# Attention and two gated products on one core: state products on row tiles, the first batch's product and the second's attention put on the job list, and softmax scalings put on ScalarE

## The chip, the core and the metric

The kernel runs on one core of one Trainium2 chip. The engines are TensorE (PE, with its weight loads PEld), VectorE (DVE), ScalarE (ACT), GpSimd (POOL), and the queue SP that issues most of the transfers. The metric is device time in microseconds, of the whole launch, as the median of several runs. Lower is better.

## The reference, cut to what matters

```python
# x: 8 x 8 x 512 x 64, state: 8 x 8 x 32 x 64 (batch, head, rows, depth)
scores  = scale * x @ state.T            # read weights a  = softmax over the 32 state rows
scores2 = scale * state @ x.T            # write weights a2 = softmax over the 512 rows
                                         # both: exp(s - max) / (sum + 1e-9)
xread, sread = a @ state, a2 @ x
X = concat([xread, sread], rows)         # 8 x (512 + 32) rows, heads side by side: 4352 x 512
X = ((X @ w1) * (X @ w2)) @ w3 @ w_out   # 512 -> 1024 -> 1024 -> 512
out = ((X @ w_a) * (X @ w_b)) @ w_out2   # 512 -> 1536 -> 512
```

The weights arrive as 64-bit floats and are converted on the chip; the output is float32.

## The kernel before, in words

**Precision.** Most products run in a reduced format, fp32r, in three passes: an operand is split into a rounded part h and a remainder l, and h·h, h·l and l·h are summed (`PASSES`). One split is a cast on ACT and a subtraction on DVE or POOL (`split` L130; the rows name the parts `wkh`, `wkl`, `ah`, `al`). Small products run in plain fp32; each of these shows as two records in the trace.

**What is multiplied.** xread is never formed for the first product. Since xread @ w = a @ (state @ w), the kernel first makes p = state @ [w1, w2] per head (`state_product` L320, tile `pb`, moved to SBUF as `sg`), stores p to DRAM (`p_d`), loads it back in another layout (`pr`), splits it, and multiplies by the read weights: ap and bp are the two products of a batch, h = ap·bp. Also w3 @ w_out is formed once (`weight_product` L362, tile `wp`, result `ws`), so that x2 = h @ ws (tile `x2p`).

**Stage one, the job list, 0 to 154.5 us.** Weight loads, conversions (two operations on ACT, two on DVE, one on POOL for each half), state products for all eight batches, w3 @ w_out, and batch 0's attention are `Job`s (L610). `EARLY` (L24) orders the loads; `run_jobs` (L653) is a planner that places the jobs with costs written in the code, gives each to an engine, and thus fixes the order on each engine and on SP. PSUM's eight banks are divided: three for `pb`, two for transposed w3, one for `wp`, two for attention. The state is laid out block-diagonally (`bdh`, `bdl`, `bd`, six tiles that are first set to zero), so that one product of 128 rows handles two heads; there are 64 such products of three passes each.

**Stage two, batches 0 to 7, 154.5 to 631.4 us.** `block1` runs eight steps per batch. A step (L1085) is six passes into ap, a copy of ap on ACT, six into bp, a multiply on DVE (`hfp`), a split, and, one step late, twelve passes into x2p (L1130). Between the passes stand small pieces of the next batches' attention: the table `MIDDLE` (L534) says which TensorE pieces come after which step, `BEHIND` (L543) which moves on ACT and DVE. `scores` is the product with the state, `maxima` to `row_split` the two softmaxes, `read` the product a2 @ x. The last batch is interleaved with the product for the state rows. Weights of stage three are converted meanwhile (`Intake`, tasks `ab`, started at the steps of `AB_AT` L37).

**Stage three, from 631.4 us.** `block2` computes the second gated product in three-pass products.

## Time and profile before

| what | value |
|---|---|
| median of 3 runs | 1415.35 us (1412.34 to 1421.07) |
| profiled execution, its time | 1415.62 us |
| its span | 1413.9 us |
| granted TensorE clock, mean over the span | 0.977 of full speed |
| busy: PE, PEld, DVE, ACT, POOL | 1342.6, 1089.4, 758.8, 540.8, 431.9 us |

Busy time is counted on the profiled execution's span; matmuls overlap a little, so PE's busy share is not its share at peak rate. An engine's idle time costs something only where TensorE waits for it. The clock is given as a share of full speed: 1.00 is 2.4 GHz, 0.5 is 1.2 GHz.

### The profile page before, as it was taken

The page shows a single profiled execution, that of the slowest core. Times are in us where ns is not written, and L with a number is a line of the kernel's source. Part 1 is how long each engine was busy: PE and PEld are TensorE (multiplying, and loading weights), DVE is VectorE, ACT ScalarE, POOL GpSimd, SP SyncE. Part 2 cuts the span into 40 slices and gives each one's busy share as a digit, 9 for nine tenths or more (in the row PEclk, how much of TensorE's full clock was granted, in tenths as well). Part 3 has the DMA queues.
Part 4 walks back from the last instruction along what each step waited for, and adds up shares of the span by engine and source line. Part 5 has one row for each costly group of instructions (what it writes and reads, how often), then busy time and mean ns, then how long its engine had stood idle before and what let it go on. Part 6 is the DMA issues. An engine that isn't in the chain of part 4 may idle for free.

```text
span 1413.9 us, 17464 instructions
## 1 busy us (share of the span) xinstructions
PE 1342.6 (95%) x6596; PEld 1089.4 (77%) x6596; DVE 758.8 (54%) x979; ACT 540.8 (38%) x915; POOL 431.9 (31%) x292
## 2 busy tenths in 40 slices
PE   6599999999899999989999999999999999999998
PEld 3377777777677677878788888888888888888877
DVE  8997377686777577756652271222462223622241
ACT  7667445545445355535422141111331223322220
POOL 4544243533453336625530043111131011311110
PEclk8699999999999999999999999999999999999999
DMA  9689732944555555256754326543464443644401
GB/s 295 195 291 314 227 121 105 283 139 172 181 175 168 155 162 130 75 196 241 258 214 144 108 103 221 189 158 128 140 226 165 154 141 133 225 164 164 150 1 60
DMA packets 120612, 242.85 MB, mean 172 GB/s; under 512 B 43984, under 2 KB 64464, under 8 KB 120528
## 3 DMA queue, kind: packets, MB, share of 16 engines
q1 hardware_dynamic: 115952, 225.48, 48.8%
q0 software_dynamic: 4576, 16.26, 3.0%
q8 instruction: 52, 0.85, 0.2%
q14 instruction: 32, 0.26, 0.1%
HBM read 176.16 MB, written 65.54 MB: 171 GB/s over the span
## 4 chain that ended last, share of the span: by engine, by line
PE 64%; DVE 6%; issue 2%; ACT 2%; DMA 1%; POOL 0%; SPq 0%; DVEq 0%; ACTq 0%; POOLq 0%
PE o L1375 18%; PE r L1363 18%; PE v L1363 9%; PE q L1363 5%; PE x2p L1130 4%; PE abs L1418 2%; PE bp L1071 2%; PE ap L1071 2%; PE os L1447 1%; PE bs L1071 1%; DVE hfp L1095 1%; DMA z<-z_d 1%; DVE ab L167 1%; DVE hp L132 1%; DVE sw L167 0%
## 5 line engine op out<-in xcount | busy, mean ns | idle before, releaser
L1375 PE MATMUL o<-z,h 128*128 128x512 f32 x1152 | 276.8, 389 | 2.9 <-DMA z<-z_d 1.6
L1375 PEld LDWEIGHTS o<-z,h 128*128 128x128 f32 x1152 | 216.0, 188 | 49.0 <-DMA z<-z_d 2.0
L1538 POOL TENSOR_TENSOR hb<-e,e 128x512 f32<-128x512 f32 x48 | 62.4, 1300 | 467.5 <-DVE e L1388 467.5
L1130 PE MATMUL x2p<-hp,ws 128*128 128x512 f32 x768 | 188.3, 394 | 2.7 <-DVE hp L132 2.2
L131 ACT CAST h<-e 128x512 fp32r<-128x512 f32 x48 | 29.8, 620 | 375.2 <-DVE e L1541 361.3
L1130 PEld LDWEIGHTS x2p<-hp,ws 128*128 128x128 f32 x768 | 145.7, 191 | 35.1 <-DVE hp L132 3.3
L1388 DVE TENSOR_TENSOR e<-e,q 128x512 f32<-128x512 f32 x48 | 33.0, 688 | 197.9 <-PE q L1363 197.9
L132 POOL TENSOR_TENSOR pl<-pr,ph 128x1024 fp32r<-128x1024 f32 x32 | 78.7, 2458 | 136.0 <-ACT ph L131 101.1
L131 ACT CAST hp<-hfp 128x512 fp32r<-128x512 f32 x64 | 39.7, 620 | 124.1 <-DVE hfp L1095 120.9
L132 DVE TENSOR_TENSOR hp<-hfp,hp 128x512 fp32r<-128x512 f32 x64 | 56.8, 887 | 48.6 <-ACT hp L131 48.0
L1388 DVE TENSOR_TENSOR e<-e,v 128x512 f32<-128x512 f32 x48 | 33.0, 687 | 82.4 <-PE v L1363 82.4
L1095 DVE TENSOR_TENSOR hfp<-asbp,bp 128x512 f32<-128x512 f32 x64 | 43.5, 679 | 54.3 <-PE bp L1071 53.2
L1363 PE MATMUL r<-xT4h,w 128*128 128x512 f32 x192 | 67.1, 390 | 2.0 <-DVE e L1388 2.0
L1363 PE MATMUL r<-xT2h,w 128*128 128x512 f32 x192 | 67.1, 390 | 0.0
L1363 PE MATMUL r<-xB11h,w 128*128 128x512 f32 x192 | 66.9, 389 | 0.0
L1363 PE MATMUL v<-xT1h,w 128*128 128x512 f32 x192 | 66.9, 389 | 0.0
L1363 PE MATMUL r<-xT3h,w 128*128 128x512 f32 x192 | 66.9, 389 | 0.0
L1363 PE MATMUL q<-xB21h,w 128*128 128x512 f32 x192 | 66.9, 389 | 0.0
L1363 PE MATMUL v<-xB22h,w 128*128 128x512 f32 x192 | 66.9, 389 | 0.0
L1089 ACT COPY asbp<-ap 128x512 f32<-128x512 f32 x64 | 37.6, 587 | 68.4 <-PE ap L1071 68.0
L1071 PE MATMUL bp<-ah,ph 128*128 128x512 f32 x128 | 57.8, 452 | 2.2 <-ACT sr L529 1.7
L132 DVE TENSOR_TENSOR h<-e,h 128x512 fp32r<-128x512 f32 x48 | 34.5, 719 | 33.4 <-ACT h L131 33.4
(506 smaller groups left out, 2996.5 us busy)
## 6 DMA issues: line engine op xcount, KB each, us to landing
w<-w_d SPq DMA_DIRECT2D x172, 512.0 KB, 5.2
w_d<-w SPq DMA_DIRECT2D x48, 512.0 KB, 2.7
p_d<-sg SPq DMA_DIRECT2D x64, 256.0 KB, 4.7
pr<-p_d SPq DMA_DIRECT2D x32, 512.0 KB, 5.1
x<-in_x_dram SPq DMA_DIRECT2D x64, 128.0 KB, 3.5
x_d<-x2sp POOLq DMA_DIRECT2D x16, 512.0 KB, 5.4
sw<-in_moe_w_dram SPq DMA_DIRECT2D x32, 256.0 KB, 6.8
xB<-x_d SPq DMA_DIRECT2D x16, 512.0 KB, 4.7
```

The lines of the kernel that those rows point to most:

```text
L131: nc.scalar.copy(hi, src)
L132: (eng or nc.vector).tensor_tensor(out=lo, in0=src, in1=hi.bitcast(F32), op=ALU.subtract)
L167: nc.vector.scalar_tensor_tensor(out=out, in0=c, scalar=0x80000000, in1=out, op0=ALU.bitwise_and, op1=ALU.bitwise_or)
L1071: nc.tensor.matmul(dst[:, :n], lhsT=l[m], rhs=r[q], start=i == 0 and j == 0, stop=i == k - 1 and j == 2,)
L1089: nc.scalar.copy(a_sb[:, :n], pa[:, :n])
L1095: nc.vector.tensor_tensor(out=hf[:, :n], in0=a_sb[:, :n], in1=pb[:, :n], op=ALU.mult)
L1130: nc.tensor.matmul(acc[j], lhsT=w_s[f][:, m, j * P : (j + 1) * P], rhs=h[:, q, :n], start=per == 1 and f == 0 and i == 0, stop=f == NF1 - ...
L1363: nc.tensor.matmul(t, lhsT=w[m], rhs=xf[g].parts[x][q][:, k, :], start=first and k == 0 and i == 0, stop=k == 1 and i == 2, skip_group_che ...
L1375: nc.tensor.matmul(t, lhsT=h[:, m, part * P : (part + 1) * P], rhs=z_t[f][:, q, :], start=first and c == 0, stop=last and c == 2,)
L1388: nc.vector.tensor_tensor(out=out, in0=x, in1=y, op=ALU.add)
L1418: nc.tensor.matmul(t[:, w * 256 : (w + 1) * 256], lhsT=l[m], rhs=x_s[k][q], start=k == 0 and i == 0, stop=k == 3 and i == 2,)
L1538: nc.gpsimd.tensor_tensor(out=h2[-1][:, f % 2, :], in0=e2, in1=e5, op=ALU.mult)
```

## The change

- **State products.** The state is transposed, copied once to one tile `stT` and not split; w1 and w2 are not split either. A product has 64 rows in the contraction (one head), the two heads of a pair stand on rows 0 to 63 and 64 to 127 of the array and write two banks, in plain fp32: 64 products in 32 pairs. Those of batches 0 to 3 are made early; the 16 pairs of batches 4 to 7 are jobs of low priority, moved by ACT alone. The stores to `p_d` are 128 of 128 KB, where there were 64 of 256 KB.
- **Order and banks.** All eight PSUM banks are one pool. `EARLY` begins with w_out and w3, so w3 @ w_out is TensorE's first large work. `KEEP`, `STORE_BEHIND`, the tables of the `ab` tasks (six from the batches' steps where there were seven) and the planner's costs change too.
- **Job list.** Batch 0's whole product (`first_product`, `first_copy`, `first_mult`, `first_high`, `first_low`, `first_output`), batch 1's attention and batch 2's transposes of x become jobs; the loop over batches begins at 1. Of batch 0, x2 is made after all eight steps, in four runs of 24 passes (tile `x2f`).
- **Scores.** Eight products per batch, each 64 rows by 32 columns of the array, into two banks, all after step 1; before, four of 128 rows by 64 columns, two after step 0 and two after step 1.
- **Softmax.** The addition of 1e-9, the scale of the maximum (`nm`) and half of x's copies go to ACT; the write weights are no longer scaled on DVE (two operations, `e<-e,r`), but their product is, when ACT moves it (`sn`, two operations where there was one).
- **Splits on POOL** of 128x1024 become two of 512 columns.

```diff
 NUNITS = 47
-BANKS = dict(pb=3, wt=2, wp=1, at=2)
+BANKS = dict(ps=8)
...
 EARLY = (
-    "wk0_0 wk1_1 wk0_1 wo0 wo1 wo3 wo2 wk1_0 x0 w3_0 w3_1 "
-    "w3_2 wk2_0 x1 w3_3 wk2_1 wk3_1 wk3_0 w3_4 w3_5 w3_6 w3_7"
+    "wo1 wo3 wo0 w3_1 wo2 w3_2 w3_0 wk0_0 x0 wk1_0 wk2_0 w3_3 "
+    "w3_5 w3_6 x1 wk1_1 w3_4 wk3_0 wk0_1 x2 w3_7 wk3_1 wk2_1"
 ).split()
...
-KEEP = 5
+KEEP = 9
 KEEP_SG = 2
-STORE_BEHIND = 24
-
-
-
-AB_AT = {0: 1, 1: 7, 2: 13, 8: 19, 9: 25, 10: 31, 11: 37}
-AB_LATER = (3, 4, 5, 6, 7)
-AB_RESERVE = 5
+KEEP_UNTIL = 40
+STORE_BEHIND = 18
+
+LATE_KEEP = 6
+LATE_PRIO = 10
...
         nc.scalar.copy(hi, src)
-        (eng or nc.vector).tensor_tensor(out=lo, in0=src, in1=hi.bitcast(F32), op=ALU.subtract)
+        if eng is nc.gpsimd and len(src.shape) == 2 and src.shape[1] == 1024:
+            parts = [slice(i * 512, (i + 1) * 512) for i in range(2)]
+        else:
+            parts = [slice(None)]
+        for i in parts:
+            (eng or nc.vector).tensor_tensor(
+                out=lo[:, i], in0=src[:, i], in1=hi[:, i].bitcast(F32), op=ALU.subtract
+            )
...
 
...
-    def state_product(p, nh, bp, i):
-        if i == 0:
-            sg[p, nh, bp] = unit(f"sg{p}_{nh}_{bp}")
-        t = pb[p, nh, bp, i] = bank(f"pb{p}_{nh}_{bp}_{i}")
-        wk = pair("wk", f"{p}_{nh}")
-        for n, (l, m) in enumerate(PASSES):
+    def state_product(p, nh, bg, i):
+
+        for r in range(2):
+            if i == 0:
+                sg[p, nh, bg, r] = unit(f"sg{p}_{nh}_{bg}_{r}")
+            t = pb[p, nh, bg, i, r] = bank(f"pb{p}_{nh}_{bg}_{i}_{r}")
+            rows = slice(r * D, (r + 1) * D)
             nc.tensor.matmul(
                 t,
-                lhsT=bd_s[p // 2][l][:, p % 2, 2 * bp : 2 * bp + 2, :],
-                rhs=wk[m][:, half[i]],
-                start=n == 0,
-                stop=n == 2,
-            )
-
-    def state_move(p, nh, bp, i, eng):
-        dst = sg[p, nh, bp].rearrange("p (q w c) -> p q w c", q=2, w=2)[:, :, i, :]
-        src = flat(pb.pop((p, nh, bp, i)), 256)
+                lhsT=st_s[rows, (bg * NP + p) * P : (bg * NP + p + 1) * P],
+                rhs=conv[f"wk{p}_{nh}"].out[rows, half[i]],
+                start=True,
+                stop=True,
+            )
+
+    def product_move(p, nh, bg, i, r, eng):
+        dst = sg[p, nh, bg, r].rearrange("p (q w c) -> p q w c", q=2, w=2)[:, :, i, :]
+        src = flat(pb.pop((p, nh, bg, i, r)), 256)
         if eng == "A":
             nc.scalar.copy(dst, src)
         else:
             nc.vector.tensor_copy(dst, src)
 
...
     def recip(s, n, tag):
         r = sm.tile([P, n], F32, tag=tag, name=tag)
-        nc.vector.tensor_scalar(out=r, in0=s, scalar1=1e-9, scalar2=None, op0=ALU.add)
+        nc.scalar.activation(out=r, in_=s, func=AF.Identity, bias=eps, scale=1.0)
         nc.vector.reciprocal(out=r, in_=r)
...
-            nc.vector.tensor_copy(self.xt[g][:, 0, :], self.banks.pop((g, 0)))
+            nc.scalar.copy(self.xt[g][:, 0, :], self.banks.pop((g, 0)))
...
+        def scores(self):
+
+            for r in range(2):
+                self.banks[r] = bank(f"st{self.b}_{r}")
+            c = self.b // 4 * 512 + self.b % 4 * NS
+            for p in range(NP):
+                for r in range(2):
+                    rows = slice(r * D, (r + 1) * D)
+                    nc.tensor.matmul(
+                        self.banks[r][NS * p : NS * (p + 1), :],
+                        lhsT=st_s[rows, c + p * P : c + p * P + NS],
+                        rhs=self.xt[p // 2][rows, p % 2, :],
+                        start=True,
+                        stop=True,
+                    )
+            free(*(f"xt{self.b}_{g}" for g in range(2)))
...
+            nc.scalar.activation(out=self.nm, in_=mx, func=AF.Copy, scale=-SCALE)
...
+        def col_sums(self):
+            self.r2 = recip(self.sum2, 2, f"r2_{self.b % 4}")
...
+            t = self.banks.pop("r")
+            for g in range(2):
+                part = slice(g * D, (g + 1) * D)
+                nc.scalar.activation(
+                    out=self.sn[:, part], in_=t[:, part], func=AF.Copy, scale=self.r2[:, g : g + 1]
+                )
...
-        0: [(1, "scores", 0)],
-        1: [(1, "scores", 1)],
+        1: [(1, "scores")],
...
-        for bp in range(B // 2):
-            moves = []
+        for bg in range(1):
+            moves = {0: [], 1: []}
             for i in range(2):
                 pr = Job(
                     "P",
-                    0.65,
-                    lambda a=(p, nh, bp, i): state_product(*a),
-                    after=[lows[i], state_done[p // 2, bp // 2]] + last[-1:],
-                    need=1 - i,
+                    1.0,
+                    lambda a=(p, nh, bg, i): state_product(*a),
+                    after=[adds[i], state_moved[bg]] + last[-1:],
+                    need=2 - 2 * i,
                     keep=KEEP_SG,
                     prio=2 + len(loads) / 100,
-                    banks=("pb", 1),
+                    banks=("ps", 2),
                 )
                 last.append(pr)
...
+                for r in range(2):
+                    moves[r].append(
+                        Job(
+                            "AV",
+                            (0.6, 0.85),
+                            lambda e, a=(p, nh, bg, i, r): product_move(*a, e),
+                            after=[pr],
+                            prio=0,
+                        ).gives("ps", 1)
+                    )
...
+    def attention_jobs(b, done):
+        prio = 1 + 2 * b
+        a = attn[b]
+        t = Job("P", 1.3, a.scores, after=[*done, *state_moved.values()], prio=prio, banks=("ps", 2))
+        for g in range(2):
+            done.append(
+                Job("A", 0.6, lambda g=g: a.scores_move(g), after=[t] + done[2:], need=1 - g, prio=prio).gives("ps", 1)
+            )
+        mx = Job("V", 2.9, a.maxima, after=done[2:], need=1, prio=prio)
+        ce = Job("A", 1.3, a.col_exp, after=[mx], need=1, prio=prio)
+        rs = Job("V", 2.9, a.row_shift, after=[mx], prio=prio)
+        re = Job("A", 1.1, a.row_exp, after=[rs], prio=prio)
+        sc = Job("V", 0.3, a.col_sums, after=[ce], prio=prio + 2)
+        su = Job("V", 1.5, a.sums, after=[re], prio=prio)
+        ct = Job("P", 1.8, a.col_transpose, after=[ce], prio=prio + 2, banks=("ps", 2))
+        cm = Job("AV", (1.3, 1.4), lambda e: a.col_move(), after=[ct, sc], need=1, prio=prio + 2).gives("ps", 2)
+        rn = Job("V", 2.9, a.row_norm, after=[su], need=1, prio=prio)
+        sp = Job("A", 1.1, a.row_split, after=[rn], need=2, prio=prio)
+        attended[b] = Job("G", 2.4, lambda: None, after=[sp], prio=prio), cm
...
+    for f in range(NF1):
+        pa = Job(
+            "P",
+            1.4,
+            lambda f=f: first_product(f, 0),
+            after=[ready[0, f // 2], attended[0][0]],
+            banks=("ps", 1),
+        )
+        ac = Job("A", 0.65, lambda f=f: first_copy(f), after=[pa] + mults[-2:-1]).gives("ps", 1)
+        pc = Job("P", 1.4, lambda f=f: first_product(f, 1), after=[pa], banks=("ps", 1))
+        mu = Job("V", 0.85, lambda f=f: first_mult(f), after=[ac, pc] + lows[-2:-1]).gives("ps", 1)
+        hi = Job("A", 0.65, lambda f=f: first_high(f), after=[mu], need=1)
+        lo = Job("V", 0.85, lambda f=f: first_low(f), after=[hi])
+        mults.append(mu)
...
+    for p in range(NP):
+        for nh in range(2):
+            products = []
+            moves = {0: [], 1: []}
+            for i in range(2):
+                last = Job(
+                    "P",
+                    1.0,
+                    lambda a=(p, nh, 1, i): state_product(*a),
+                    after=[last],
+                    need=2 - 2 * i,
+                    keep=LATE_KEEP,
+                    prio=LATE_PRIO,
+                    banks=("ps", 2),
+                )
+                products.append(last)
+                for r in range(2):
+                    moves[r].append(
+                        Job(
+                            "A", 0.6, lambda a=(p, nh, 1, i, r): product_move(*a, "A"), after=[last], prio=4
+                        ).gives("ps", 1)
+                    )
+            frees_after(products, f"wk{p}_{nh}")
...
+    moves = []
+    for j in range(4):
+        o = Job("P", 5.5, lambda j=j: first_output(j), after=lows + w_done + moves[-2:-1], prio=8, banks=("ps", 1))
```

**TensorE's first work.** Before, after the state's transposes `stT`, state products in three passes, ordered by the arrival of their halves `wkh` and `wkl`:

```order
L259 MATMUL stT_159<-ident,st_147 128x128 x4
L326 MATMUL pb_0_0_0_200<-wkh_0_187,bdh_121 128x512
L326 MATMUL pb_0_0_0_200<-wkl_0_188,bdh_121 128x512
L326 MATMUL pb_0_0_0_200<-wkh_0_187,bdl_123 128x512
L326 MATMUL pb_0_0_1_237<-wkh_0_187,bdh_121 128x512
L326 MATMUL pb_0_0_1_237<-wkl_0_188,bdh_121 128x512
L326 MATMUL pb_0_0_1_237<-wkh_0_187,bdl_123 128x512
```

After, the same place; `w3t` is transposed w3, `wp` the product w3 @ w_out:

```order
L267 MATMUL stT_150<-ident,st_138 128x128 x4
L347 MATMUL w3t_0_260<-ident,w_1_218 128x128 x4
L347 MATMUL w3t_1_267<-ident,w_1_218 128x128 x4
L347 MATMUL w3t_0_312<-ident,w_2_254 128x128 x4
L347 MATMUL w3t_1_323<-ident,w_2_254 128x128 x4
L361 MATMUL wp_334<-woh_227,w3h_273 128x512
L361 MATMUL wp_334<-wol_228,w3h_273 128x512
L361 MATMUL wp_334<-woh_227,w3l_274 128x512
```

The state products now stand behind the first weight products, and TensorE's first large work takes `w3h` and `woh` where it took `wkh` and `bdh`.

**TensorE in batch 0's product, after.** `f_0` and `f_1` are the two products of one step, formerly ap and bp; `pb` now belongs to batches 4 to 7:

```order
L1054 MATMUL f_0_1304<-ah_765,pl_0_1229 128x512
L1054 MATMUL f_1_1322<-ah_765,ph_0_1228 128x512
L1054 MATMUL f_1_1322<-al_766,ph_0_1228 128x512
L1054 MATMUL f_1_1322<-ah_765,pl_0_1229 128x512
L318 MATMUL pb_1_1_0_0_1340<-wk_1_957,stT 128x512
L318 MATMUL pb_1_1_0_1_1343<-wk_1_957,stT 128x512
L318 MATMUL pb_1_1_1_0_1352<-wk_1_957,stT 128x512
L318 MATMUL pb_1_1_1_1_1354<-wk_1_957,stT 128x512
L1054 MATMUL f_2_1358<-ah_765,ph_1_1311 128x512
```

Fourteen pairs of this kind stand between the first pass of batch 0's product and batch 1's first pass, and none stood there before. Each pair's two products name one `wk` tile, of which they use the two halves of the rows.

**DVE in a batch's steps 2 to 4, before.** `hfp` is the multiply of a step, `hp` its remainder, the rest the next batch's softmaxes:

```order
L426 TENSOR_REDUCE mx<-s_1935 128x2
L428 TENSOR_SCALAR nm<-mx 128x2
L432 STREAM_TRANSPOSE t_2080<-s_1935 128x1024
L1095 TENSOR_TENSOR hfp_3_2134<-asbp_3_2101,bp_3_2127 128x512
L132 TENSOR_TENSOR hp_3_2136<-hfp_3_2134,hp_3_2136 128x512
L451 TENSOR_REDUCE m<-t_2080 128x32
L452 TENSOR_TENSOR t_2080<-t_2080,m 128x1024
L384 TENSOR_SCALAR r_2142<-sum_2120 128x2
L385 RECIPROCAL r_2142<-r_2142 128x2
L463 TENSOR_SCALAR e_2119<-e_2119,r_2142 128x512 x2
```

After, the same place:

```order
L423 TENSOR_REDUCE mx<-s_1829 128x2
L427 STREAM_TRANSPOSE t_1903<-s_1829 128x1024
L1078 TENSOR_TENSOR hfp_3_1953<-asbp_3_1924,bp_3_1946 128x512
L142 TENSOR_TENSOR hp_3_1955<-hfp_3_1953,hp_3_1955 128x512
L446 TENSOR_REDUCE m<-t_1903 128x32
L447 TENSOR_TENSOR t_1903<-t_1903,m 128x1024
L377 RECIPROCAL r_2_1961<-r_2_1961 128x2
L1078 TENSOR_TENSOR hfp_4_1998<-asbp_4_1986,bp_4_1991 128x512
```

The scale of the maximum, the addition before the reciprocal and the two scalings of `e` left DVE; the reciprocal now follows an ACT instruction.

**ACT at the same place.** `asbp` is the copy of ap. Before:

```order
L1089 COPY asbp_3_2101<-ap_3_2094 128x512
L438 ACTIVATE e_2119,sum_2120<-s_1935,nm 128x512 x2
L520 COPY sn<-sr_2032 128x128
L1089 COPY asbp_4_2168<-ap_4_2161 128x512
L457 ACTIVATE t_2080<-t_2080 128x1024
```

After:

```order
L136 CAST ph_2_1892<-pr_2_1559 128x1024
L425 ACTIVATE nm<-mx 128x2
L1072 COPY asbp_3_1924<-ap_3_1917 128x512
L433 ACTIVATE e_1942,sum_1943<-s_1829,nm 128x512 x2
L376 ACTIVATE r_2_1961<-sum_1943,eps 128x2
L513 ACTIVATE sn<-sr_1863,r_1_1280 128x64 x2
L1072 COPY asbp_4_1986<-ap_4_1979 128x512
```

`nm` and the addition for `r` now stand in ACT's order ahead of the copies of steps 3 and 4, and each waits for DVE or for the exponential just ahead.

## Rows read from the trace of the kernel before

**Rows 1.** Stages by engine: start:end, length, busy us, PEclk, DMA share, GB/s.
```profile
0.00:154.50 154.50, 121.75 (x514) 92.32 (x515) 130.15 (x184) 104.22 (x191) 71.45 (x56) 0.87 0.85 274
154.50:204.10 49.60, 48.50 (x278) 37.45 (x278) 30.04 (x38) 22.40 (x38) 17.75 (x11) 1.00 0.53 155
204.10:537.10 333.00, 314.45 (x1785) 241.98 (x1784) 237.31 (x297) 162.82 (x269) 137.30 (x85) 0.97 0.55 170
537.10:631.40 94.30, 84.59 (x484) 74.06 (x483) 64.55 (x72) 46.99 (x78) 50.09 (x29) 0.96 0.44 125
631.40:1413.90 782.50, 773.36 (x3541) 643.58 (x3540) 296.79 (x390) 204.37 (x339) 155.36 (x113) 1.00 0.46 159
```

**Rows 2.** The page, busy time: engine, us, share, instructions.
```profile
PE 1342.6 (95%) x6596; PEld 1089.4 (77%) x6596; DVE 758.8 (54%) x979; ACT 540.8 (38%) x915; POOL 431.9 (31%) x292
```

**Rows 3.** Waits of PE, 0:154.5: waited for, us in all, times, longest.
```profile
PE pb L326 <- DVE wkl L312: 8.8, 6, 3.1
PE pb L326 <- ACT wkh L306: 8.6, 4, 3.4
PE st L410 <- DVE xt L404: 7.2, 1, 7.2
```

**Rows 4.** Groups on DVE, 0:154.5: names, shapes, busy us, mean ns, idle before.
```profile
L340 DVE COPY sg<-pb 128x512 f32<-128x512 f32 x23 | 15.4, 684 | 1.9 <-PE pb L326 1.9
L312 DVE TENSOR_TENSOR wkl<-wk,wkh 128x512 fp32r<-128x512 f32 x12 | 9.0, 754 | 0.2
L312 DVE TENSOR_TENSOR wol<-wo,woh 128x512 fp32r<-128x512 f32 x6 | 4.1, 683 | 0.0
L275 DVE TENSOR_TENSOR bdl<-stT,bdh 64x256 fp32r<-64x256 f32 x8 | 3.4, 421 | 2.0 <-ACT bdh L273 2.0
L404 DVE COPY xt<-xt 128x512 f32<-128x512 f32 x4 | 2.7, 681 | 0.0
L225 DVE MEMSET bdl<- 128x1024 f32 x2 | 1.8, 912 | 0.3 <-issue 0.3
L277 DVE COPY bd<-stT 64x256 f32<-64x256 f32 x4 | 1.7, 420 | 0.0
L452 DVE TENSOR_TENSOR t<-t,m 128x1024 f32<-128x1024 f32 x1 | 1.3, 1303 | 0.0
L463 DVE TENSOR_SCALAR e<-e,r 128x512 f32<-128x512 f32 x2 | 0.9, 484 | 0.0
```

**Rows 5.** Groups on ACT, 0:154.5.
```profile
L338 ACT COPY sg<-pb 128x512 f32<-128x512 f32 x41 | 23.1, 593 | 11.0 <-PE pb L326 8.8 <-issue 1.4 <-ACT w3h L306 0.4
```

**Rows 6.** DMA, 0:154.5: all bytes, then issues with KB, us to landing.
```profile
DMA packets 22435, 42.28 MB, mean 274 GB/s; under 512 B 12336, under 2 KB 12336, under 8 KB 22425
p_d<-sg SPq DMA_DIRECT2D x64, 256.0 KB, 4.7
```

**Rows 7.** Chain of waits, 370:392: start, us, what ran, records.
```profile
373.10 1.36 PE ap L1071 x6
374.46 1.01 PE st L410 x4
377.06 2.72 PE x2p L1130 x12
```

**Rows 8.** Groups over the whole span, forms apart.
```profile
L384 DVE TENSOR_SCALAR r<-sum 128x32 f32<-128x32 f32 x8 | 11.3, 1418 | 0.3
L428 DVE TENSOR_SCALAR nm<-mx 128x2 f32<-128x2 f32 x8 | 8.6, 1070 | 0.3
L520 ACT COPY sn<-sr 128x128 f32<-128x128 f32 x8 | 2.1, 258 | 0.0
```

**Rows 9.** Waits of PE, batches 1 to 6.
```profile
PE xt L399 <- DVE hfp L1095: 5.2, 3, 3.1
```

**Rows 10.** Timeline of POOL and DVE near 358: start, us, instruction.
```profile
357.64 2.40 POOL L132 TENSOR_TENSOR al<-a,ah 128x1024 fp32r<-128x1024 f32 x1 [8.23 <-ACT ah L131]
358.12 2.47 DVE L132 TENSOR_TENSOR z<-ab8t,z 128x512 fp32r<-128x512 f32 x1 [1.64 <-ACT z L131]
```

More of the change, by code (lines that the diff above doesn't have):

```diff
@@ L678, in load_job @@
     def load_job(time, go, need, lag=1.0):
[L679 removed]
+        j = Job("D", time, go, behind=loads[-1:], need=need, keep=KEEP if len(loads) < KEEP_UNTIL else 1, prio=len(loads), lag=lag)
         loads.append(j)
@@ L891, in attention_moe_moe2, with load_columns @@
-    run_jobs()
-    for e in through:
-        through[e] = max(through[e], clock[e])
-    now[0] = clock["P"]
-    for i in range(4):
-        free_pair("wo", i)
-    free(*(f"{v}{i}" for v in ("bdh", "bdl") for i in range(2)))
-    def load_columns(name, pair, f, by_head):
+                read_jobs(b)
+    def load_columns(name, pair, f):
         out = []
@@ new lines, in first_move, with first_store @@
+    def first_move(j, eng):
+        if j % 2 == 0:
+            first_t[0] = flat(unit("x2f"), 512)
+        (nc.scalar.copy if eng == "A" else nc.vector.tensor_copy)(first_t[0][:, j % 2, :], pb.pop(("x2", j)))
+    def first_store(j):
+        nc.gpsimd.dma_start(out=x2_d[0][:, j - 1 : j + 1], in_=first_t[0])
+        free("x2f", at=until[0] + 4)
+    for j in products:
+        j.after += wo_done
+    frees_after(products, *(f"wo{q}{i}" for q in "hl" for i in range(4)))
+    ready = {}
+    last = None
@@ new lines, in attention_moe_moe2 @@
+    for b, qs in ((0, range(4)), (1, range(3))):
+        for q in qs:
+            l = Job(
+                "D",
+                1.5,
+                lambda b=b, q=q: load_p(b, q),
+                after=stores[q // 2] + ([last] if last else []),
+                need=1,
+                prio=1 + 20 * b,
+                lag=1.0,
+            )
+            if b == 0 or q == 0:
+                sp = Job("A", 1.1, lambda b=b, q=q: split_p(b, q), after=[l], need=2, prio=0 + 5 * b)
+                ready[b, q] = last = Job("G", 2.4, nothing, after=[sp], prio=0 + 5 * b)
@@ new lines, in attention_moe_moe2 @@
+    moves = []
+    for j in range(4):
+        o = Job("P", 5.5, lambda j=j: first_output(j), after=lows + w_done + moves[-2:-1], prio=8, banks=("ps", 1))
+        if j == 3:
+            o.frees(*(f"fh{f}" for f in range(NF1)))
+        moves.append(
+            Job("AV", (0.6, 0.7), lambda e, j=j: first_move(j, e), after=[o], need=1 - j % 2, prio=4).gives("ps", 1)
+        )
+        if j % 2:
+            moves.append(Job("G", 0.1, lambda j=j: first_store(j), after=moves[-2:], prio=4))
+    warm_up(N_WARM[0])
@@ L1265, in attention_moe_moe2 @@
+    run_jobs()
+    for e in through:
+        through[e] = max(through[e], clock[e])
+    now[0] = clock["P"]
     chunks = [(b, q) for b in range(B) for q in range(4)]
```

285 lines of the change are left out of this document (134 added, 151 removed).

## The prediction

> **What bounds the kernel now.** I read the stage table first [rows 1], because the change touches three of its five stages. Two of them are TensorE at its peak: batch 0 takes 49.6 us with 48.5 busy, and stage three has 773 of 782 us busy at clock 1.00. Two are not. In the first 154.5 us TensorE is busy 121.8 us at a granted clock of 0.87, while DVE is busy 130.2 (84%), ACT 104.2 (67%) and the DMA engines 0.85 of the time. The six batches from 204.1 to 537.1 us hold the work of batch 0 six times and take 333.0 us, not 6 x 49.6 = 297.6: 35.4 us are lost there, with DVE busy 71% and ACT 49%. The page gives PE 95% [rows 2], an average that hides both.
>
> Then the waits of the first stage [rows 3]. State products wait 8.8 us for the remainder of w1 and w2, made by DVE, and 8.6 for the rounded part, made by ACT; scores wait 7.2 us in one piece for the copy of transposed x on DVE. So conversion on DVE bounds that stage most, ACT next. The groups on DVE [rows 4] say with what. In the batches the longest wait is for x's transposes, 5.2 us in three times, behind `hfp` on DVE [rows 9]: attention pieces queue ahead of what TensorE needs.
>
> **First stage.** I start from DVE's 130.2 us and count what has gone when batch 0's product begins. The moves `sg`: 23 on DVE now, 7 after, 16 x 0.684 = 10.9. The remainders `wkl`: 9.0. Four zero fills at 0.912: 3.6. `bdl` 3.4, `bd` 1.7. Half of x's copies: 2.7 go, but batch 2's transposes now come here, 2 x 0.68, leaving 1.4. Two scalings of `e`: 0.9 (all [rows 4]). Sum 30.9. Added: one more `wol`, 0.7, and batch 1's softmaxes, which now run before batch 0's product: seven passes over 128x1024, the longest 1.30, 8.6 in all, and 1.2 of copy and reciprocals. That leaves 130.2 - 30.9 + 0.7 + 9.8 = 109.8 us. At the share of today, 84%, the first product of batch 0 starts at 109.8 / 0.842 = 130 us, where it started at 154.5.
>
> A second route gives nearly the same. The stage moves 42.28 MB at 274 GB/s, of it 64 stores of 256 KB [rows 6]. Half of these bytes, 8.4 MB, now leave after batch 0 has begun: 33.9 / 0.274 = 124 us. I take 130, the later of the two.
>
> From there to batch 1 TensorE has work enough: 96 passes for the two products and 96 for x2 at 0.227 us (1.36 us for 6, 2.72 for 12 [rows 7]), 43.6 us, and 14 late pairs of state products. No row shows two products on different rows of the array. The nearest is a pair on different columns, 1.01 us together [rows 7], so bounds are 1.01 if the rows run side by side and 2.02 if one after the other. I take 1.01, since the two cases differ only in which edge of the array is shared: 14.1 us. With batch 0's idle 1.1 us the sum is 58.8, and batch 1 begins at 189 instead of 204.1: **-15 us**. If DVE reached 95% the product would start at 116 (-30); if it fell to 75%, at 146 (0).
>
> The late pairs stand in place of passes that leave the first stage (192 of 0.227 us, 43.6, go for 32 pairs of 1.01, 32.3). Their moves are on ACT alone, 28 x 0.593 = 17 us [rows 5] within 59 us; batch 0's own ACT work is 22.4 [rows 1], so ACT is at 66% there and hides them. The 128 stores cost SP twice as many issues; they stand behind the loads that the product waits for, and I put them at nothing, +3 at worst.
>
> **Batches 1 to 6.** Off DVE go, per batch, two copies of x (2 x 0.68), `nm` 1.07, the addition for `r` 1.42 (128x32 form) and two scalings 0.97 [rows 4, 8]: 4.8 us, 29 of 237 in six batches, so DVE falls from 71% to 63%. What moves to ACT is small (the copy `sn` of this kind took 0.26 us [rows 8]): ACT goes from 49% to about 52%. The splits on POOL are halved: now an `al` of 2.40 us on POOL stands beside a subtraction on DVE that takes 2.47 [rows 10], where an undisturbed one of this size takes 0.68 (`wol` [rows 4]). After it, the next pass of x's transposes was late. With half pieces DVE comes in between sooner. How much of the 35.4 us comes back no row says: nothing to 30. If waiting goes as u/(1-u), it falls from 2.45 to 1.70, by 31%, or 11 us; with the POOL pieces I take **-14**.
>
> The scores of a batch are two such pairs, 2 x 1.01; the eight small products can run as one group of 1.01, or 2.02 if rows don't overlap: **-6** for six batches, bounds -6 and 0. They ask for two banks at once; the ring had a dedicated pair before. A late bank costs at most what x's transposes waited, 3.1 us [rows 9]; I take 0.5 per batch: **+3**.
>
> `nm` and the addition now stand in ACT's order ahead of the copies of ap in steps 3 and 4 and wait for DVE, and DVE's reciprocal waits for ACT. The copy feeds `hfp`, and x2's passes come a step later, so there is about a step (six passes, six, twelve: 5.4 us [rows 7]) of cover: nothing, up to 1 us per batch if the cover is short.
>
> The Trainium skill, ScalarE: Activation LUTs, section Rules for kernel authors, speaks against this part: additions and multiplications belong on VectorE, not on ScalarE. The rows here disagree for these tiny shapes: 1.07 and 1.42 us on DVE, 0.26 on ACT. By the rule the batches would lose about 0.5 us each instead, and the sum below would be 1400.
>
> **The rest.** The last batch with the state block loses some DVE and POOL load: **-2** (±5). Stage three inherits one more weight task, **+1** (0 to +3).
>
> The sum against the profiled execution's own 1415.6 us (0.3 above the median, so I don't correct): 1415.6 - 15 - 14 - 6 + 3 - 2 + 1 = 1382.6. **Predicted: 1382 us.** A measurement here tells about 1% from no change, 14 us.
>
> **Rivals.**
>
> *More than this.* DVE fills 91% of the first stage (product at 120, -25), 25 us come back in the batches, and no bank is late: 1415.6 - 25 - 25 - 6 - 2 + 1 = 1359. For it: 8.8 + 8.6 + 7.2 us of waits that the change removes at the root. Chance 0.15.
>
> *Row tiles don't run side by side.* Then each late pair takes 2.02 and scores gain nothing: +14 and +6, 1402. Against it: the column pairs do. Chance 0.08.
>
> *ACT sets the pace, not DVE.* Before batch 0's product stand on ACT: 104.2 us, less 12 moves `sg` (7.1) and 16 casts `wkh` at the same 0.593 (9.5) [rows 5], less 12 block-diagonal pieces at DVE's 0.42 (5.0) [rows 4], with eight copies of x and of the state (4.7) and batch 1's attention (nine pieces of 512 columns at 0.593 and seven small ones at 0.26, 7.1): 94.4 us. If ACT keeps its share of 67%, the product starts at 140, batch 1 at 199 (-5). If the batches too give nothing back, because the work only changes the engine: 1415.6 - 5 - 6 + 3 - 2 + 1 = 1407. The Trainium skill, TensorEngine Tiling (Array Packing), section Performance Considerations, warns of this: tiling makes TensorE faster, not the emptying of PSUM. The trace bears it out so far as 64 moves stay 64. Against it: DVE, not ACT, is the fuller engine in both stages [rows 1]. Chance 0.10.
>
> *Slower: the common bank ring.* A pair holds two of eight banks until ACT has moved both, and TensorE executes in order, so a late move stops the next pass, whatever it belongs to. Each of the 14 late pairs and six scores then waits for a move behind ACT's other work. At the longest wait seen, 3.1 us [rows 9], 20 places cost 62 us: 1382 - 3 + 62 = 1441. It passes 1429.5, 1% slower, from 2.5 us per place. Against it: ACT has spare time. Chance 0.07.
>
> **How the numbers follow.** My case keeps 0.60. Its own bounds reach from 1352 to 1403. The range 1352 to 1409 takes in the first three rivals at their own times and leaves out the last and a tenth of the tails. Faster by over 1% (under 1401): 0.58 + 0.15 + half of 0.08 + a tenth of 0.10 = 0.78. Within 1%: 0.15. Slower: 0.07.
>
> **What would show it.** The first passes of batch 0 near 130 us and batch 1's near 189; no wait of TensorE for `wkh` or `wkl`, few before scores; a pair of state products at 1.0 us with both starting within 10 ns; batches 1 to 6 near 53 us each, DVE at about 62% there. If the first product comes before 120 us the first rival is right; if it comes after 138 and the batches keep 55 us, the third; pairs of 2.0 us, the second; many TensorE waits for ACT moves with a bank behind them, the last. If the batches keep their 55.5 us although DVE there has fallen, their loss is not DVE's load but the order, and the second term of my sum is wrong.

## The result, and the profile after

The changed kernel takes **1377.6 us** (median of 4 runs, 1375.6 to 1379.8), the kernel before 1414.4 (4 runs). The ratio is 0.9736, 95% interval 0.971 to 0.9763. The forecast was 1382 us, 1352 to 1409. The profiled execution of the changed kernel has a span of 1376.4 us, 37.5 less than before, at a mean granted clock of 0.983.

The stages by engine, columns as in [rows 1]. The borders are TensorE's first pass of batch 0's product, of batch 1, of batch 7 and of stage three:

```profile
0.00:135.00 135.00, 94.08 (x507) 63.09 (x507) 117.79 (x144) 91.29 (x171) 61.28 (x49) 0.87 0.77 238
135.00:199.90 64.90, 62.14 (x249) 41.77 (x249) 15.39 (x18) 31.14 (x57) 17.69 (x14) 0.95 0.60 177
199.90:504.30 304.40, 295.10 (x1821) 233.85 (x1820) 204.02 (x249) 174.53 (x309) 149.49 (x122) 1.00 0.60 196
504.30:593.00 88.70, 83.64 (x483) 73.69 (x483) 57.17 (x70) 43.77 (x73) 48.58 (x35) 0.96 0.38 125
593.00:1376.40 783.40, 773.85 (x3542) 643.56 (x3540) 303.19 (x400) 210.05 (x348) 168.16 (x135) 1.00 0.46 161
```

Against [rows 1] the first stage is 19.5 us shorter, batch 0 is 15.3 longer, batches 1 to 6 are 28.5 shorter, batch 7 with the state block 5.6 shorter, stage three 0.9 longer. Together -37.4, which is the span's difference. 2.7 us of the batches' 28.5 are only moved across a border: batch 0 now ends with its own x2, where before its last twelve passes stood in batch 1.

TensorE's waits up to 135 us, and then in batch 0's product, columns as in [rows 3]:

```profile
PE w3t L347 <- POOL w L185: 28.1, 5, 14.6
```

```profile
PE f L1054 <- ACT ph L136: 4.4, 2, 3.4
PE f L1054 <- POOL pl L142: 1.7, 3, 0.7
```

The waits for `wkh` and `wkl` are gone. In their place TensorE waits 28.1 us at the start for the first blocks of w3. From 40 to 199.9 us (the same view as the stage table, cut there) it is busy 146 of 160 us.

The wait of 3.4 us in the second list ends at 135.0 us, with the first pass, so it belongs to the first stage; 2.6 us of waits lie inside the product. Behind it the granted clock is at its lower level. The first pass, and the stretch to 140.8 us in the stage table's columns:

```profile
135.00 0.79 PE L1054 MATMUL f<-ah,ph 128*128 128x512 f32 x1 [3.44 <-ACT ph L136]
135.00:140.80 5.80, 5.67 (x13) 3.86 (x14) 0.75 (x2) 4.16 (x9) 5.02 (x4) 0.50 0.73 190
```

Twelve passes take 5.8 us there, where 12 at 0.227 us [rows 7] are 2.7. In the kernel before the clock was 1.00 in all of batch 0 [rows 1].

In batches 1 to 6 the wait that led [rows 9], 5.2 us for x's transposes, is nearly gone:

```profile
PE xt L391 <- DVE hfp L1078: 0.2, 1, 0.2
```

TensorE's idle time there fell from 18.5 to 9.3 us, a third of the 28.5. The rest is busy time, 19.4 us less: 2.7 moved across the border, some 6 in the scores, and most of what is left goes with the clock, 0.97 in these batches before [rows 1] and 1.00 now. In the kernel before it stood at 0.50 in four stretches of 17 us together, which cost up to half of that; each began in or just behind TensorE's waits. The longest one, while TensorE waited 3.1 us for x's transposes [rows 9]:

```profile
363.80:370.50 6.70, 5.27 (x16) 4.22 (x17) 5.62 (x9) 3.21 (x5) 3.62 (x2) 0.50 0.77 284
```

TensorE's row tiles, as the timeline shows them: start, length, instruction, records. An fp32 product has two records. First one pair of state products, then the eight scores:

```profile
182.37 1.13 PE L318 MATMUL pb<-wk,stT 64*128 64x512 f32 x4
...
204.20 1.09 PE L407 MATMUL st<-xt,stT 64*32 64x512 f32 x16
```

In the pair, the two first records start 7 ns apart, the two second ones 0.53 us later, and the next pass begins 1.06 us after the first; a pair on two column tiles took 1.01 [rows 7]. The eight scores start 7 ns apart from each other, and the next pass begins 1.02 us after the first of them, where four took two times 1.01. So tiles on different rows do run side by side, and the second rival is out.

### The profile page after: what moved, and what is told of

Read it like the earlier page. It is cut to its first block, busy times and chain, and to the rows that moved or that the text cites. A ratio compares the mean times of both kernels' runs of the same rounds, so it can differ in the third digit from the quotient of the medians.

```text
span 1376.4 us, 17480 instructions
## 1 busy us (share of the span) xinstructions
PE 1308.8 (95%) x6596; PEld 1056.0 (77%) x6596; DVE 697.6 (51%) x879; ACT 550.8 (40%) x955; POOL 445.2 (32%) x353
## 4 chain that ended last, share of the span: by engine, by line
PE 70%; DVE 5%; ACT 2%; issue 2%; DMA 1%; POOL 1%; SPq 0%; DVEq 0%; POOLq 0%; ACTq 0%
PE o L1512 19%; PE r L1500 18%; PE v L1500 9%; PE x2p L1113 6%; PE q L1500 5%; PE bp L1054 3%; PE ap L1054 3%; PE abs L1555 2%; PE os L1584 1%; DVE sw L179 1%; PE x2s L1113 1%; DMA w_d<-w 1%; DMA z<-z_d 1%; PE as L1054 1%; PE bs L1054 1%
## 5 line engine op out<-in xcount | busy, mean ns | idle before, releaser
L1113 PE MATMUL x2p<-hp,ws 128*128 128x512 f32 x672 | 161.9, 390 | 0.0
L1113 PEld LDWEIGHTS x2p<-hp,ws 128*128 128x128 f32 x672 | 125.7, 188 | 26.3
L142 POOL TENSOR_TENSOR pl<-pr,ph 128x512 fp32r<-128x512 f32 x64 | 85.6, 1357 | 114.7 <-ACT ph L136 99.5
L1078 DVE TENSOR_TENSOR hfp<-asbp,bp 128x512 f32<-128x512 f32 x56 | 38.2, 682 | 77.7 <-PE bp L1054 76.0
L136 ACT CAST hp<-hfp 128x512 fp32r<-128x512 f32 x56 | 34.7, 619 | 81.4 <-DVE hfp L1078 78.9
L142 DVE TENSOR_TENSOR hp<-hfp,hp 128x512 fp32r<-128x512 f32 x56 | 46.8, 836 | 40.0 <-ACT hp L136 38.6
L1054 PE MATMUL bp<-ah,ph 128*128 128x512 f32 x112 | 48.7, 435 | 5.0 <-DVE hfs L1078 3.1
L1072 ACT COPY asbp<-ap 128x512 f32<-128x512 f32 x56 | 32.8, 585 | 46.2 <-PE ap L1054 46.1
```

Of the source, the lines that this page charges most:

```text
L136: nc.scalar.copy(hi, src)
L142: (eng or nc.vector).tensor_tensor(out=lo[:, i], in0=src[:, i], in1=hi[:, i].bitcast(F32), op=ALU.subtract)
L1054: nc.tensor.matmul(dst[:, :n], lhsT=l[m], rhs=r[q], start=i == 0 and j == 0, stop=i == k - 1 and j == 2,)
L1072: nc.scalar.copy(a_sb[:, :n], pa[:, :n])
L1078: nc.vector.tensor_tensor(out=hf[:, :n], in0=a_sb[:, :n], in1=pb[:, :n], op=ALU.mult)
L1113: nc.tensor.matmul(acc[j], lhsT=w_s[f][:, m, j * P : (j + 1) * P], rhs=h[:, q, :n], start=per == 1 and f == 0 and i == 0, stop=f == NF1 - ...
```

## The experiments

The stages of each kernel, read from its trace at the same borders, in us:

| kernel | product 0 starts | batch 0 | batches 1 to 6 | batch 7 and state | ratio to before (95%) |
|---|---|---|---|---|---|
| before | 154.5 | 49.6 | 333.0 | 94.3 | 1 |
| the change | 135.0 | 64.9 | 304.5 | 88.7 | 0.9736 (0.971 to 0.9763) |
| scalings on DVE | 137.5 | 63.4 | 307.3 | 87.6 | 0.9766 (0.9749 to 0.9783) |
| POOL pieces whole | 134.8 | 63.8 | 313.1 | 87.1 | 0.9791 (0.9771 to 0.981) |
| both undone | 137.2 | 65.2 | 319.9 | 87.0 | 0.9874 (0.9859 to 0.989) |
| before with both | 155.1 | 48.9 | 314.5 | 98.5 | 0.9904 (0.9887 to 0.992) |
| seven weight tasks | 135.6 | 64.3 | 301.3 | 94.6 | 0.9878 (0.9861 to 0.9894) |
| old order of loads | 132.6 | 71.0 | 306.3 | 86.8 | 0.9783 (0.9763 to 0.9803) |
| DVE relieved | 132.9 | 65.4 | 306.0 | 88.7 | 0.9738 (0.9723 to 0.9752) |
| planner's delays | 136.8 | 63.6 | 304.2 | 86.8 | 0.975 (0.9727 to 0.9774) |
| one pass, changed | 135.4 | 63.6 | 306.2 | 86.9 | 0.9744 (0.9716 to 0.9771) |
| one pass, before | 149.3 | 53.4 | 330.7 | 95.6 | 0.9993 (0.9979 to 1.0007) |
| weight product in pieces | 130.9 | 65.3 | 304.6 | 86.8 | 0.9711 (0.9683 to 0.9738) |
| all products early | 141.0 | 77.2 | 305.9 | 86.8 | 0.9872 (0.9843 to 0.9901) |

Batches 1 to 6 of the changed kernel are between 304 and 306.5 us in every kernel that leaves them alone, so some 2 us is what one profile can tell there. The four kernels near 306 have one stretch of 3.4 us at a granted clock of 0.50 late in batch 6, the others none.

### What quickened the batches

**Scalings back on DVE.** In `recip`, `maxima` and `col_sums`; with it `read_move` and the copies of x go back to the code of before:

```diff
-        nc.scalar.activation(out=r, in_=s, func=AF.Identity, bias=eps, scale=1.0)
+        nc.vector.tensor_scalar(out=r, in0=s, scalar1=1e-9, scalar2=None, op0=ALU.add)
...
-            nc.scalar.activation(out=self.nm, in_=mx, func=AF.Copy, scale=-SCALE)
+            nc.vector.tensor_scalar(
+                out=self.nm, in0=mx, scalar1=-SCALE, scalar2=None, op0=ALU.mult
+            )
...
+            for g in range(2):
+                e = flat(self.e2, S)[:, g, :]
+                nc.vector.tensor_scalar(
+                    out=e, in0=e, scalar1=r[:, g : g + 1], scalar2=None, op0=ALU.mult
+                )
```

> The changed kernel with the softmax scalings put back on DVE: the addition of 1e-9, the scale of the maximum, both copies of transposed x, and the two scalings of e instead of the scaled move of sn. Theory A (DVE's load sets the loss in batches 1 to 6): some 5 us of DVE work per batch come back, batches 1 to 6 take 12 us or more longer than 304 us, the whole about 1390 us. Theory B (POOL's long pieces block DVE): the POOL pieces stay halved, so the batches lose 4 us at most, the whole about 1381 us.

Measured 1380.9 us. The batches grow by 2.8 us, although DVE is busy 221.7 us in them where it was 204.0: nearer to theory B than to A, and little more than one profile can tell. DVE's load by itself is not what TensorE waits for.

**POOL's pieces whole.**

```diff
-        if eng is nc.gpsimd and len(src.shape) == 2 and src.shape[1] == 1024:
+        if False:
```

> The changed kernel with the splits on POOL in one piece of 128x1024 again. Theory B: DVE's subtractions beside them go back from about 1.4 to 2.5 us, batches 1 to 6 take about 10 us longer, the whole about 1388 us. Theory A: 3 us at most, about 1380 us.

Measured 1384.3 us, batches +8.6: theory B, within its size. The groups on DVE in batches 1 to 6 (forms apart), of the changed kernel, and then with whole pieces:

```profile
L142 DVE TENSOR_TENSOR z<-ab11t,z 128x512 fp32r<-128x512 f32 x1 | 1.7, 1684 | 1.1 <-ACT z L136 1.1
L142 DVE TENSOR_TENSOR z<-ab9t,z 128x512 fp32r<-128x512 f32 x1 | 1.4, 1369 | 1.6 <-ACT z L136 1.6
L142 DVE TENSOR_TENSOR z<-ab2t,z 128x512 fp32r<-128x512 f32 x1 | 1.2, 1162 | 1.0 <-ACT z L136 1.0
```

```profile
L142 DVE TENSOR_TENSOR z<-ab9t,z 128x512 fp32r<-128x512 f32 x1 | 2.5, 2474 | 1.6 <-ACT z L136 1.6
L142 DVE TENSOR_TENSOR z<-ab10t,z 128x512 fp32r<-128x512 f32 x1 | 2.5, 2462 | 1.7 <-ACT z L136 1.7
```

The reader is to see the mean: a subtraction of 512 columns that met a 2.40 us piece on POOL took 2.47 before [rows 10], takes 1.2 to 1.7 beside half pieces, and 2.5 again beside whole ones. TensorE itself loses on two accounts, which the stage table's row of these batches shows:

```profile
198.60:511.70 313.10, 299.93 (x1821) 237.31 (x1820) 207.24 (x249) 174.61 (x309) 140.03 (x85) 0.98 0.60 191
```

It is idle 13.2 us instead of 9.3, and busy 4.8 us longer with the same passes, at a granted clock of 0.98 instead of 1.00. More than half of the price is thus the clock, not the waits.

**Both undone.** The edits of the two together.

> The changed kernel with both undone, the scalings on DVE and the POOL pieces whole. Each alone lengthened batches 1 to 6 by 2.8 and 8.6 us. If they act apart, 11 us together, the whole about 1388 us. If DVE's load and POOL's long pieces act through each other, which is what theory A's queue would give, 18 us or more, the whole about 1395 us or more.

Measured 1395.8 us, the batches +15.4: more than the sum of the two (11.4), less than the 18 that a queue would give. The two act through each other, by about 4 us in the batches, and by 8 us in the whole (+3.3 and +6.7 alone, +18.2 together). A likely way is that a DVE with more to do meets POOL's long pieces more often: in the batches it is busy 204.0 us in the changed kernel, 221.7 and 207.2 with one part undone, and 235.8 with both, 11 more than the two add up to.

**The kernel before with both.** The edits in reverse, on the kernel before.

> The kernel before with only these two parts of the change: scalings to ACT and POOL's splits in halves. If they are what quickened the batches, its batches 1 to 6 go from 333 to about 310 us, the whole to about 1392 us. If the rest of the change (order, scores in one go, bank pool) carries it, 333 to about 322 us, the whole about 1403 us.

Measured 1400.6 us. Batches 1 to 6 alone (columns of the stage table):

```profile
204.00:518.50 314.50, 306.54 (x1785) 238.72 (x1784) 198.52 (x252) 173.10 (x304) 146.60 (x122) 0.99 0.58 179
```

From 333.0 to 314.5 us is -18.5, near the first theory. The time as a whole went by only -14, since batch 7 took 98.5 us instead of 94.3. So the two small parts make 15 to 18 of the 28.5 us, from either side.

**Seven weight tasks inside the batches.**

```diff
-AB_AT = {0: 9, 1: 14, 2: 20, 9: 26, 10: 32, 11: 38}
-AB_LATER = (3, 4, 5, 6, 7, 8)
+AB_AT = {0: 9, 1: 14, 2: 19, 8: 24, 9: 29, 10: 34, 11: 39}
+AB_LATER = (3, 4, 5, 6, 7)
```

> The changed kernel with seven weight tasks of stage three inside the batches, as in the kernel before, evenly spaced from step 9 to 39, and five later. Theory C (the batches are quicker because one conversion left them): batches 1 to 6 take 6 to 8 us longer, the whole about 1383 us or the same if stage three gives it back. Theories A and B: the batches take at most 3 us longer, the whole 1377 to 1380 us.

Measured 1396.5 us, a time that none of the theories gave: the batches took 301.3 us, none the longer. Batch 7 with the state block took 94.6, as in the kernel before, and stage three 798.3, which is 14.9 more than in the changed kernel. TensorE's waits from 510 us on:

```profile
PE r L1500 <- ACT e L1640: 8.1, 1, 8.1
PE o L1512 <- DMA z<-z_d: 5.1, 1, 5.1
```

One task less inside the batches is thus the likeliest cause of batch 7's 5.6 us. Why the seventh costs stage three so much here and not in the kernel before (782.5 us) stays open: the steps of the tasks and the reserve of buffers differ too.

### What held the first stage

**Old order of loads.** `EARLY` of the kernel before, with `x2` behind `wk3_0`.

> The changed kernel with the order of early loads of the kernel before (w1 and w2 first, batch 2's x added behind the last of them). Theory D (DVE's conversion work sets when batch 0's product can begin, whatever comes first): batch 1 starts within 5 us of 200, the whole 1373 to 1383 us. Theory E (TensorE's 39 us without work at the start, waiting for the first transposed w3, are lost for good): TensorE starts earlier, batch 1 at about 188, the whole about 1366 us.

Measured 1383.4 us; batch 1 starts at 203.6. Within theory D's 5 us, and against E, as TensorE's wait only changed its place:

```profile
PE pb L318 <- POOL wk L185: 21.0, 6, 12.4
```

The product started at 132.6 us, earlier than in the changed kernel, but here TensorE is busy all the time from there to batch 1, so in this order its own work sets the end:

```profile
132.60:203.60 71.00, 71.00 (x305) 52.08 (x305) 22.34 (x28) 34.01 (x63) 17.61 (x14) 0.98 0.31 98
```

**DVE relieved.** Moves of state products on ACT alone, remainders of w_out on POOL alone:

```diff
-                            "AV",
-                            (0.6, 0.85),
-                            lambda e, a=(p, nh, bg, i, r): product_move(*a, e),
+                            "A",
+                            0.6,
+                            lambda a=(p, nh, bg, i, r): product_move(*a, "A"),
...
-                    "VG",
-                    (0.85, 1.5),
...
+                    "G",
+                    1.5,
...
```

> The changed kernel with DVE relieved in the first stage alone: its seven moves of state products go to ACT and its seven remainders of w_out to POOL, 9.9 us by the rows of the changed kernel. Theory D (DVE, 98% busy from 10 to 130 us, sets the start of batch 0's product): the start moves from 135 to about 126 us, the whole to about 1369 us. Rival F (what follows the last conversion, ACT's moves, the stores and loads of p and the POOL splits, sets it): the start stays within 3 us of 135, the whole 1376 to 1382 us.

Measured 1376.6 us. The start moved by 2.1 us for 9.9 us of relief, so rival F. Up to 132.9 us DVE is busy 110.7 us instead of 117.8, and POOL 72.6 instead of 61.3. (From 10 to 130 us DVE was busy 95% in the changed kernel, not 98%.) SP's waits (before the load named) show where it went:

```profile
SPq L151 <- POOL wk L185: 8.7, 1, 8.7
```

Loads waited on POOL, which frees their buffers and now had the remainders too. So this run doesn't show what a relief of DVE without a load on POOL would give.

**Planner's delays.** `lag=5.0` for an early store of p and `lag=4.0` for a load of p, where 2.0 and 1.0 stood.

> The changed kernel with two delays of the planner set to what the trace shows: a store of p 5 us and a load of p 4 us until it can be used, where 2 and 1 stood. Four more pairs of late state products then stand ahead of batch 0's product. If the wait of 3.4 us before it and the 6.1 us of waits for split pieces inside it are time that other work can fill, batch 0 takes about 58 us instead of 64.9 and the whole about 1371 us; if the waits only move, the whole stays within 3 us of 1377.

Measured 1378.9 us: the waits only moved. Batch 0 took 63.6 us, but its start came 1.8 later, and with ten late pairs in it instead of 14 TensorE was idle 6.9 us there instead of 2.8.

**One pass of w3 @ w_out**, in the changed kernel and in the kernel before (two thirds of the product's passes are left out):

```diff
-            for n, (l, m) in enumerate(PASSES):
+            for n, (l, m) in enumerate(PASSES[:1]):
```

> The changed kernel without two of the three passes of w3 @ w_out: 128 of its 192 passes, 29 us of TensorE's work ahead of batch 0's product, are left out and nothing else moves (the product is then less exact). Theory H (from 40 us on TensorE's own work, 146 of 160 us busy, sets when batch 1 starts): batch 1 starts 15 to 25 us earlier than 199.9, the whole about 1357 us. Rival F (conversions, and then the way of p through DRAM, set it): batch 1 starts within 4 us of 199.9, the whole above 1372 us.

> The kernel before without the same 128 passes. The prediction's theory (DVE bounds the whole first stage of the kernel before): batch 0 starts within 4 us of 154.5, the whole above 1410 us. Theory H for the kernel before (TensorE's backlog bounds the end of the stage, busy 10 of 10 us from 120 us on): batch 0 starts 12 us or more earlier, the whole about 1400 us or less.

Measured 1378.5 and 1413.2 us. I had come to theory H because TensorE is nearly full from 40 us on; it falls. With 29 us of work taken away batch 1 starts at 199.0 instead of 199.9, and in the kernel before at 202.7 instead of 204.1; there batch 0 started 5.2 earlier, between the two theories, and took 3.8 longer. Ahead of the product TensorE was busy because it had work to fill the time, not because the time depended on it. Its wait in the changed kernel simply grew:

```profile
PE w3t L347 <- POOL w L185: 42.0, 9, 14.6
```

SP's timeline says what does not move. Changed kernel: start, time of the group, line, transfer, count:

```profile
106.06 22.02 SPq L336 DMA_DIRECT2D p_d<-sg  x24
128.18 0.39 SPq L593 DMA_DIRECT2D pr<-p_d  x1
129.79 7.37 SPq L336 DMA_DIRECT2D p_d<-sg  x8
137.26 0.38 SPq L593 DMA_DIRECT2D pr<-p_d  x1
137.74 8.96 SPq L336 DMA_DIRECT2D p_d<-sg  x16
146.80 0.38 SPq L593 DMA_DIRECT2D pr<-p_d  x1
147.28 5.36 SPq L336 DMA_DIRECT2D p_d<-sg  x8
152.68 0.98 SPq L593 DMA_DIRECT2D pr<-p_d  x2
```

and with one pass:

```profile
106.27 22.60 SPq L336 DMA_DIRECT2D p_d<-sg  x24
128.97 0.39 SPq L593 DMA_DIRECT2D pr<-p_d  x1
137.69 0.39 SPq L593 DMA_DIRECT2D pr<-p_d  x1
147.56 0.39 SPq L593 DMA_DIRECT2D pr<-p_d  x1
```

SP issues them in the kernel's order. The first load of p, `pr`, stands behind 24 stores, which wait for moves of the state products, and goes at 128.2 us, or 129.0 with one pass. By the kernel's code eight of the 24 write what this load reads. They go as soon as ACT has moved their products, behind a wait of 8.2 us (first line, SP's waits from 95 to 160 us), and eight others go between them and the load:

```profile
SPq L336 <- ACT sg L330: 12.0, 2, 8.2
120.49 3.83 SPq L336 DMA_DIRECT2D p_d<-sg  x8
124.43 3.65 SPq L336 DMA_DIRECT2D p_d<-sg  x8
```

The last of its own stores landed at 126.3, so SP's order costs the first load some 2 us, and the moves ahead of it more. The next loads go at 137.3, 146.8 and 152.7, behind 8, 16 and 8 stores, of which only eight of the 16 write what the load reads. Each load releases two of batch 0's eight steps. That is why the product starts at 135, whatever TensorE has to do ahead of it. Its length is another matter: of the 64.9 us TensorE is busy 62.1, the first 5.8 at half clock, and it waits 2.6 for p. The kernel before had the same row of events, and removing passes left it where it was; first the kernel before, then with one pass:

```profile
130.83 11.78 SPq L344 DMA_DIRECT2D p_d<-sg  x12
142.70 0.54 SPq L600 DMA_DIRECT2D pr<-p_d  x1
```

```profile
142.66 0.39 SPq L600 DMA_DIRECT2D pr<-p_d  x1
```

There TensorE is busy without a gap from the first load of p at 142.7 to 154.5, mostly with the weight product; in the changed kernel that is finished at 125.7.

**All state products early.** `range(2)` for `range(1)` in `early_wk`, and no late pairs. (Six of the 32 pairs still came behind the first pass of batch 0's product.)

> The changed kernel with the state products of all eight batches made early, as in the kernel before, so that no late pairs stand in batch 0's product. Theory H: the pairs are the same work for TensorE wherever they stand; batch 0's product starts about 14 us later and takes about 14 us less, the whole within 4 us of 1377. Rival F: the doubled stores and moves ahead of batch 0's product delay it by 20 us or more, the whole 1383 us or more.

Measured 1396.2 us: rival F again, with the start only 6.0 us later but batch 0 12.3 longer. SP has 32 stores ahead of the first load of p, and 32 more ahead of the third:

```profile
114.58 21.01 SPq L336 DMA_DIRECT2D p_d<-sg  x32
135.69 0.39 SPq L593 DMA_DIRECT2D pr<-p_d  x1
136.18 8.26 SPq L336 DMA_DIRECT2D p_d<-sg  x16
144.48 0.44 SPq L593 DMA_DIRECT2D pr<-p_d  x1
161.21 15.63 SPq L336 DMA_DIRECT2D p_d<-sg  x32
176.93 3.53 SPq L593 DMA_DIRECT2D pr<-p_d  x6
```

So making half of the state products late is worth 18.6 us, and not for the sake of TensorE's time: in batch 0 it waits 16.8 us in one piece for the third load. How much of that is SP's order and how much ACT's moves no run separates. Ahead of the third load SP waits 16.2 us for a move on ACT, and then takes 15.6 us for 32 stores, 16 of which write what that load reads.

**Weight product in pieces.** The first two weight products in four pieces each, the third in two, by the block of w_out that each needs, and `w3_1 wo1 w3_2 wo3 wo0 w3_0 wo2` at the head of `EARLY`:

```diff
+            for n, ws in enumerate(pieces):
+                ks = [2 * w + q for w in ws for q in range(2)]
+                wpj = Job(
+                    "P",
+                    5.5 * len(ks) / 8,
+                    lambda i=i, a=(ks, n == 0, n == len(pieces) - 1): weight_product(i, *a),
+                    after=list(lows) + ([wpj] if wpj else []),
...
```

> The changed kernel with the first three weight products cut into pieces by the w_out block they need, and w3's first blocks loaded ahead, so that TensorE can begin 60 of these passes (13.6 us) before all of w_out is converted. Theory H: the work that TensorE does before 40 us is missing later, batch 1 starts 5 to 10 us earlier, the whole about 1370 us. Rival F: batch 1 starts within 3 us of 199.9, the whole 1375 to 1381 us.

Measured 1374.0 us (1372.3 to 1374.5), 3.6 below the changed kernel and the best of all, but the two ratios' intervals overlap, so better than the change is likely and not shown. Batch 1 starts 3.8 us earlier, between the two theories, with the product 4.1 us earlier. Since the order of the loads changed with it, the gain may be the order's.

## Why the prediction was right or wrong

The direction and the time were right, 1382 against 1377.6, but by two errors of opposite sign and nearly one size, which is luck: the first stage gave 10.8 us less than forecast, batches 1 to 6 gave 11.5 more (-17 forecast), and batch 7 3.6 more.

- **First stage, -15: measured -4.2** (batch 1 at 199.9 for 204.1). This is the step that failed. The product's start was worked out as DVE's work at DVE's present share, and came at 135.0 instead of 130; the other 6.1 us are batch 0's, below. Part of it is size: DVE had 117.8 us before the product, not 109.8, which at the share of 84% would even be 140. The 8.0 us are conversions. The 40 `shift` operations of the second kind (two inputs) lasted longer; the kernel before, then the change (busy time of that line on DVE):

```profile
0.00:154.50 154.50, 37.60 (x40) 0.87 0.85 274
```

```profile
0.00:135.00 135.00, 44.28 (x40) 0.87 0.77 238
```

 That is 6.7 us more for the same operations, and the other line of the conversion has 1.2 more. One of these operations takes 0.69 us by itself and 1.65 to 1.71 when it meets an operation on POOL; 17 of the 40 were that long, where 10 were before:

```profile
105.07 0.69 DVE L179 SCALAR_TENSOR_TENSOR w<-w_7r,w 128x512 uint32<-128x512 uint32 x1
105.90 1.38 POOL L185 TENSOR_TENSOR w<-w,w_7r 128x512 int32<-128x512 int32 x1 [1.15 <-DMA wk_1r<-in_moe_w_dram]
106.14 1.69 DVE L179 SCALAR_TENSOR_TENSOR wk<-wk_1r,wk 128x512 uint32<-128x512 uint32 x1
```

 The other part is the mechanism. Taking 9.9 us of work off DVE gave 2.1, though with more work on POOL. The start follows the way of p: the last conversions and state products, ACT's moves, SP's stores and loads, the split. Before, this way was hidden behind the weight product. I had put the 128 stores "at nothing, +3 at worst", and the way that they are on sets the start. No run took load off ACT alone. With the scalings back on DVE, ACT had 4.2 us less before the product and DVE 8.4 more, and the start came 2.5 later, so ACT's load by itself is unlikely to be the bound.
- **Batch 0 in 58.8 us: measured 64.9.** TensorE's passes were sized right for full clock (14 pairs took 13.3 us, forecast 14.1). Of the 6.1 us some 3 are the clock, at 0.50 up to 140.8 us behind the wait for `ph`; the sum had no term for it. TensorE's idle time is 2.8 us, nearly all of it waits for `ph` and `pl` inside the product, where the sum had 1.1. Some 2 us are not accounted for.
- **Batches, -14 for DVE and POOL, -6 for scores, +3 for the ring: measured -28.5**, or -25.8 without the moved border. Scores: -1.0 per batch, as forecast. So row tiles were priced right from pairs of columns. DVE's relief and POOL's halves: 15 to 18 us, so the term's mechanism was right and its size somewhat small; but the halves carried more of it than the scalings, against the weight I gave them. The forecast counted waits alone; a good part came as clock, 0.97 to 1.00. No late bank shows among the batches' waits, so the +3 is not there. Some 2 to 5 us are not accounted for.
- **Scalings on ACT.** The tiny operations take 0.20 and 0.32 us on ACT (groups over the span), where DVE took 1.07 and 1.42 [rows 8]:

```profile
L376 ACT ACTIVATE r<-sum,eps 128x32 f32<-128x32 f32 x8 | 2.6, 322 | 5.1 <-DVE sum L459 5.1
L425 ACT ACTIVATE nm<-mx 128x2 f32<-128x2 f32 x8 | 1.6, 204 | 9.8 <-DVE mx L423 9.8
```

 The rule of the Trainium skill (ScalarE: Activation LUTs, Rules for kernel authors) would have put them on DVE; with them there the batches took 2.8 us longer, so the trace goes against the rule here, though by little more than one profile can tell. The waits that ACT gained (9.8 us before `nm` in eight batches) cost TensorE nothing that shows.
- **Batch 7, -2: measured -5.6**, most likely through the weight task that left. **Stage three, +1: measured +0.9.**
- **Rivals.** Row tiles run side by side, and state products waited 1.7 us in all for moves of other tiles, in the first stage alone: the second and the last are out. ACT was busy 68% before batch 0's product, as it had been, and batch 1 began at 199.9 us, where the third rival had 199 (with the product at 140, not 135), but the batches went the other way. The rule of the Trainium skill (TensorEngine Tiling (Array Packing), Performance Considerations) that tiling doesn't speed up the emptying of PSUM is borne out so far as SP's stores wait 12.0 us for ACT's moves from 95 to 160 us, 8.2 of them ahead of stores that the first load of p reads.
